# Re-tiling a gated linear attention with a leaky feed-forward into units of one batch and one chunk, with one activation-table set, on one core

## The chip, the core and the metric

The kernel runs on one core of a Trainium2 chip. The metric is the time of one execution on the device, in microseconds (us), where less is better. "Timed" means that figure; "span" means the length of the profiled execution, which is about two us shorter. With one core there is no neighbouring die to compare, so a run counts as slow only when it lies over 1.5% above the fastest of its own kernel.

Engines are named as the profile names them: PE is TensorE's matmul stream, PEld its weight loads, DVE is VectorE, ACT is ScalarE, POOL is GpSimd, SP is SyncE (here it only issues transfers). L89 is line 89 of the kernel concerned. A "unit" below is one batch of one chunk of 128 time steps, with all 8 heads; there are 24 units.

## The reference

```python
# q, k, v, f_logit: (4 batches, 8 heads, 768 steps, 48); all float32
f = 1.0 / (1.0 + np.exp(-f_logit))
for t in range(S):
    state = f[:, :, t, :, None] * state + k_t (outer) v_t      # 48 x 48 per batch and head
    y[:, :, t] = q_t @ state
x = y.transpose(0, 2, 1, 3).reshape(3072, 384)                 # tokens x (heads * 48)
h = x @ w_in                                                   # 384 -> 2048
out = np.maximum(0.01 * h, h) @ w_out                          # 2048 -> 384, float32 out
```

Both kernels work in chunks of 128 steps. Within a chunk, the gates are summed in log space by a matmul with a triangular matrix (`cs`). The queries are then scaled by exp(-cs) and the keys by exp(cs). After a transpose, masked score matmuls (`pw`, `wm`) and a carried state replace the loop over steps.

## The kernel before

One iteration handles one chunk of all 32 batch-head pairs. These are the parts that the argument touches (cuts marked `...`):

```python
    # three per-head tiles, each head padded from 48 to 128 columns
    lf = statep.tile([128, NJ, 128], BF16, tag="lf")           # NJ = 32
    qh = statep.tile([128, NJ, 128], BF16, tag="qh")
    kh = statep.tile([128, NJ, 128], BF16, tag="kh")
    ...
        for kk in range(3):                                    # weights: SyncE loads, ScalarE casts
            stg = wstage.tile([128, FF], FP32, tag="wstg")
            nc.sync.dma_start(out=stg, in_=moe_w_in[kk * 128:(kk + 1) * 128, :])
            nc.scalar.copy(out=w_in_b[:, kk, :], in_=stg)
    ...
        for p in range(4):                                     # emit_attn(c)
            nc.scalar.activation(t_b[:, js, :], f_raw[:, js, :], AF.Exp, scale=-1.0)
            nc.scalar.activation(lf[:, js, 0:D], t_b[:, js, :], AF.Ln, bias=1.0)
            nc.tensor.matmul(cs, ut, lf[:, js, 0:D], start=True, stop=True)
            nc.scalar.activation(a_t[:, js, :], cs, AF.Exp, scale=-1.0)
            nc.scalar.activation(em_t[:, js, :], cs, AF.Exp, scale=1.0)
            ...
        for b in range(4):
            ...                                                # 16 transposes, 8 scores, 16 py per batch
            nc.scalar.copy(out=xnat, in_=py)
            nc.sync.dma_start(out=x_dram[c][b * C:(b + 1) * C, :], in_=xnat)
        ...
        for kk in range(3):                                    # x goes through DRAM to be transposed
            nc.sync.dma_start_transpose(xt, x_dram[c][:, kk * 128:(kk + 1) * 128])

    def emit_moe(c, xts):                                      # 512 tokens at once
        for ff in range(16):
            for kk in range(3):
                nc.tensor.matmul(pm, w_in_b[:, kk, ff * 128:(ff + 1) * 128], xts[kk], ...)
            nc.scalar.activation(gT[:, ff, :], pm, AF.Prelu, alpha=0.01)
        ...
```

Attention of chunk c+1 is emitted before the feed-forward of chunk c.

Of the kernel before, what the change touches and what calls it, by code (L numbers as in the profile page):

```python
# [8 lines left out]
FP32 = mybir.dt.float32  # L10
BF16 = mybir.dt.bfloat16
AF = mybir.ActivationFunctionType


@with_exitstack
def kernel(
# [16 lines left out]
    NJ = B * H  # L33
    KD, FF = moe_w_in.shape

    const = ctx.enter_context(tc.tile_pool(name="const", bufs=1))
    wpool = ctx.enter_context(tc.tile_pool(name="wpool", bufs=1))
    wstage = ctx.enter_context(tc.tile_pool(name="wstage", bufs=1))
    statep = ctx.enter_context(tc.tile_pool(name="statep", bufs=1))
    inp = ctx.enter_context(tc.tile_pool(name="inp", bufs=2))  # L40
    work = ctx.enter_context(tc.tile_pool(name="work", bufs=2))
    xtp = ctx.enter_context(tc.tile_pool(name="xtp", bufs=2))
    gpool = ctx.enter_context(tc.tile_pool(name="gpool", bufs=2))
    opool = ctx.enter_context(tc.tile_pool(name="opool", bufs=4))
    dram = ctx.enter_context(tc.tile_pool(name="dram", bufs=1, space=bass.MemoryType.DRAM))

    ps_cs = ctx.enter_context(tc.tile_pool(name="ps_cs", bufs=1, space=bass.MemoryType.PSUM))
    ps_tp = ctx.enter_context(tc.tile_pool(name="ps_tp", bufs=1, space=bass.MemoryType.PSUM))
    ps_w = ctx.enter_context(tc.tile_pool(name="ps_w", bufs=1, space=bass.MemoryType.PSUM))
    ps_y = ctx.enter_context(tc.tile_pool(name="ps_y", bufs=2, space=bass.MemoryType.PSUM))  # L50
    ps_m = ctx.enter_context(tc.tile_pool(name="ps_m", bufs=3, space=bass.MemoryType.PSUM))
# [7 lines left out]

    state_f = statep.tile([128, NJ, D], FP32, tag="state_f")  # L60
    state_b = statep.tile([128, NJ, D], BF16, tag="state_b")
    nc.vector.memset(state_f, 0.0)
    nc.vector.memset(state_b, 0.0)
    lf = statep.tile([128, NJ, 128], BF16, tag="lf")
    qh = statep.tile([128, NJ, 128], BF16, tag="qh")
    kh = statep.tile([128, NJ, 128], BF16, tag="kh")
    nc.vector.memset(lf[:, :, D:128], 0.0)
    nc.vector.memset(qh[:, :, D:128], 0.0)
    nc.vector.memset(kh[:, :, D:128], 0.0)

    if True:
        w_in_b = wpool.tile([128, 3, FF], BF16, tag="w_in")
        for kk in range(3):
            stg = wstage.tile([128, FF], FP32, tag="wstg")
            nc.sync.dma_start(out=stg, in_=moe_w_in[kk * 128:(kk + 1) * 128, :])
            nc.scalar.copy(out=w_in_b[:, kk, :], in_=stg)
        w_out_b = wpool.tile([128, 16, KD], BF16, tag="w_out")
        for kk in range(4):
            stg = wstage.tile([128, 4, KD], FP32, tag="wstg")
            src = moe_w_out[kk * 512:(kk + 1) * 512, :].rearrange(  # L80
                "(a p) n -> p a n", p=128)
            nc.sync.dma_start(out=stg, in_=src)
            nc.scalar.copy(
                out=w_out_b[:, 4 * kk:4 * kk + 4, :], in_=stg)

    x_dram = [dram.tile([4 * C, KD], BF16, name=f"xdram{c}", tag=f"xdram{c}")
              for c in range(NCH)]

    qv = q.rearrange("b h (nc t) d -> nc t (b h) d", t=C)  # L89
    kv = k.rearrange("b h (nc t) d -> nc t (b h) d", t=C)  # L90
    vv = v.rearrange("b h (nc t) d -> nc t (b h) d", t=C)
    fv = f_logit.rearrange("b h (nc t) d -> nc t (b h) d", t=C)
# [5 lines left out]
    def emit_attn(c):  # L98
        xts_out = []
        q_raw = inp.tile([128, NJ, D], FP32, tag="q_raw")  # L100
        k_raw = inp.tile([128, NJ, D], FP32, tag="k_raw")
        v_raw = inp.tile([128, NJ, D], FP32, tag="v_raw")
        f_raw = inp.tile([128, NJ, D], FP32, tag="f_raw")
        for p in range(4):
            nc.sync.dma_start(out=f_raw[:, 8 * p:8 * p + 8, :],  # L105
                              in_=fv[c, :, 8 * p:8 * p + 8, :], )
        nc.sync.dma_start(out=q_raw, in_=qv[c])
        nc.sync.dma_start(out=k_raw, in_=kv[c])
        nc.sync.dma_start(out=v_raw, in_=vv[c])

        t_b = work.tile([128, NJ, D], BF16, tag="t_b")
        a_t = work.tile([128, NJ, D], BF16, tag="a_t")
        em_t = work.tile([128, NJ, D], BF16, tag="em_t")

        for p in range(4):
            js = slice(8 * p, 8 * p + 8)
            nc.scalar.activation(t_b[:, js, :], f_raw[:, js, :], AF.Exp,  # L117
                                 scale=-1.0)
            nc.scalar.activation(lf[:, js, 0:D], t_b[:, js, :], AF.Ln,  # L119
                                 bias=1.0)  # L120
            cs = ps_cs.tile([128, 8 * D], FP32, tag="cs")
            nc.tensor.matmul(cs, ut, lf[:, js, 0:D], start=True, stop=True)  # L122
            nc.scalar.activation(a_t[:, js, :], cs, AF.Exp, scale=-1.0)  # L123
            nc.scalar.activation(em_t[:, js, :], cs, AF.Exp, scale=1.0)  # L124
            nc.vector.tensor_mul(qh[:, js, 0:D], q_raw[:, js, :],  # L125
                                 a_t[:, js, :])
            nc.vector.tensor_mul(kh[:, js, 0:D], k_raw[:, js, :],  # L127
                                 em_t[:, js, :])

        v_b = work.tile([128, NJ, D], BF16, tag="v_b")  # L130
        nc.scalar.copy(out=v_b, in_=v_raw)  # L131

        if c < NCH - 1:
            csa = ps_cs.tile([128, NJ], FP32, tag="cs")
            for j in range(NJ):
                mm(csa[:, j:j + 1], lf[:, j, :], ones_col, j, NJ)
            A_sb = work.tile([128, NJ], FP32, tag="A_sb")
            nc.scalar.activation(A_sb[0:D, :], csa[0:D, :], AF.Exp,
                                 scale=-1.0)

        qkT = work.tile([128, 2, NJ, 128], BF16, tag="qkT", bufs=1)
        for b in range(4):
            for qk, src in enumerate((qh, kh)):
                tp = ps_tp.tile([128, 8, 128], BF16, tag="tp")
                for hh in range(8):
                    j = 8 * b + hh
                    mm(tp[:, hh, :], src[:, j, :], ident, hh, 8, tr=True)
                nc.vector.tensor_copy(out=qkT[:, qk, 8 * b:8 * b + 8],  # L148
                                      in_=tp)

            wms = []
            for g in range(2):
                pw = ps_w.tile([128, 4, 128], FP32, tag="pw")
                for hh in range(4):
                    j = 8 * b + 4 * g + hh
                    mm(pw[:, hh, :], qkT[:, 1, j, :],
                       qkT[:, 0, j, :], hh, 4)
                wm = work.tile([128, 4, 128], BF16, tag="wm", bufs=4)
                nc.vector.tensor_mul(wm, pw,  # L159
                                     ut[:, None, :].to_broadcast([128, 4, 128]))  # L160
                wms.append(wm)

            py = ps_y.tile([128, 8, D], FP32, tag="py")
            ny = 16 if c > 0 else 8
            if c > 0:
                for hh in range(8):
                    mm(py[:, hh, :], qkT[:, 0, 8 * b + hh, :],
                       state_b[:, 8 * b + hh, :], hh, ny)
            for hh in range(8):
                j = 8 * b + hh  # L170
                mm(py[:, hh, :], wms[hh // 4][:, hh % 4, :], v_b[:, j, :],
                   (ny - 8) + hh, ny)
            xnat = xtp.tile([128, KD], BF16, tag="xnat", bufs=4)
            nc.scalar.copy(out=xnat, in_=py)  # L174
            with tc.high_priority(offset=20000):
                nc.sync.dma_start(out=x_dram[c][b * C:(b + 1) * C, :],
                                  in_=xnat)


        if c < NCH - 1:  # L180
            for b in range(4):
                pt = ps_cs.tile([128, 8, D], FP32, tag="cs", name="pt")
                for hh in range(8):
                    j = 8 * b + hh
                    mm(pt[:, hh, :], kh[:, j, :], v_b[:, j, :], hh, 8)
                ss = slice(8 * b, 8 * b + 8)
                nc.vector.tensor_add(state_f[0:D, ss, :], state_f[0:D, ss, :],
                                     pt[0:D, :, :])
                nc.vector.tensor_mul(
                    state_f[0:D, ss, :], state_f[0:D, ss, :],  # L190
# [70 lines left out]
```

## Time and profile before

| | before |
|---|---|
| timed, median of 4 (range) | 263.91 us (263.54 to 265.58) |
| profiled span | 260.9 us |
| TensorE / ScalarE / VectorE / GpSimd busy | 200.2 / 171.4 / 128.4 / 1.1 us |
| activation-table loads | 35 of 1283 ns = 44.9 us of ScalarE |
| first feed-forward matmul | 62.20 us |

These lines come from the page of the kernel before. The first is busy time with its share of the span. Then come rows of 40 equal slices of the span, each digit the busy share in tenths. Of these, PEclk is the clock granted to TensorE, again in tenths. The chain that ended last follows, then two groups of instructions (count, total busy us, mean ns, then idle time before them).

```profile
PE 200.2 (77%) x1921; PEld 125.9 (48%) x1944; DVE 128.4 (49%) x233; ACT 171.4 (66%) x269; POOL 1.1 (0%) x9
...
PE   0013686016999967955998999996999999999994
...
ACT  3997249994889955899735978469764285505800
...
PEclk9999999555999997995799999999899999999999
...
PE 42%; ACT 33%; DMA 12%; SPq 6%; issue 3%; DVE 2%
...
L119 ACT ACT_TABLE_LOAD x17 | 21.8, 1283 | 0.3
...
L117 ACT ACT_TABLE_LOAD x11 | 14.1, 1283 | 0.2
```

TensorE is busiest over the whole run, but not throughout, and the chain that ended last gives TensorE 42% and ScalarE 33% of the span. TensorE's row is nearly empty (0 1) in the eighth and ninth slices, where ScalarE's row reads 9 9 and the granted clock 5. The windows view says the same in us. Its columns are the stretch, its length, busy us (with instruction count) of PE, PEld, DVE, ACT and POOL, the granted clock, the DMA share (which can pass 1) and GB/s:

```profile
20.00:45.00 25.00, 15.79 (x185) 12.85 (x184) 16.35 (x30) 14.72 (x19) 0.00 (x0) 1.00 0.70 173
45.00:60.00 15.00, 1.97 (x12) 0.72 (x13) 3.63 (x8) 14.55 (x19) 0.00 (x0) 0.51 0.59 101
60.00:80.00 20.00, 18.12 (x164) 10.59 (x167) 8.44 (x15) 14.29 (x23) 0.00 (x0) 0.86 1.04 189
```

From 45 to 60 us TensorE works 1.97 of 15 us while ScalarE works 14.55 us, much of that on table loads: Exp, Ln and the other functions alternate, and each alternation reloads a table. The clock of 0.51 beside that idle stretch agrees with the Trainium skill, "TensorE: Matmul & The Clock Gate", Part 1, which says that the array falls back to half its clock after an idle window of about 3.4 us. As an estimate, TensorE's busy time multiplied by (1 - granted clock), summed over nine windows of the run, gives 11 us of extra matmul time from a lowered clock.

### The profile page before, as it was taken

What the parts mean: (1) busy time and instruction counts of PE and PEld (TensorE: products, weight loads), DVE (VectorE), ACT (ScalarE), POOL (GpSimd) and SP (SyncE); (2) the same over time, 40 slices, a digit from 0 to 9 for tenths busy, and PEclk for the clock granted to TensorE, in tenths of its full rate; (3) what the DMA queues carried; (4) which work ended last, traced back from release to release, by engine and by line L of the source; (5) the groups of instructions that cost most, each with busy time, mean ns of one, the idle gap of its engine ahead of it and who ended that gap; (6) DMA issues with size and microseconds to landing.
All of it is one profiled execution on the core that took longest, in us unless ns stands there. A gap on an engine that the chain in (4) does not pass through costs nothing.

```text
span 260.9 us, 4667 instructions
## 1 busy us (share of the span) xinstructions
PE 200.2 (77%) x1921; PEld 125.9 (48%) x1944; DVE 128.4 (49%) x233; ACT 171.4 (66%) x269; POOL 1.1 (0%) x9
## 2 busy tenths in 40 slices
PE   0013686016999967955998999996999999999994
PEld 0002575003467634743464775654765557564462
DVE  7112759212359854872314995265892387320011
ACT  3997249994889955899735978469764285505800
POOL 1000000000000000000000000000000000000000
PEclk9999999555999997995799999999899999999999
DMA  7990898099599799980999999999002401141011
GB/s 215 191 271 6 228 235 222 23 167 221 102 226 165 135 203 179 139 136 0 169 165 235 199 156 171 184 206 186 18 30 52 136 10 33 33 121 60 3 60 60
DMA packets 118244, 34.90 MB, mean 134 GB/s; under 512 B 109648, under 2 KB 117840, under 8 KB 117840
## 3 DMA queue, kind: packets, MB, share of 16 engines
q1 hardware_dynamic: 118224, 34.61, 68.2%
q8 instruction: 15, 0.25, 0.4%
q14 instruction: 5, 0.04, 0.1%
HBM read 25.17 MB, written 7.08 MB: 124 GB/s over the span
## 4 chain that ended last, share of the span: by engine, by line
PE 42%; ACT 33%; DMA 12%; SPq 6%; issue 3%; DVE 2%
PE pm L208 14%; ACT L119 6%; ACT L117 4%; PE tp L95 4%; DMA stg<-in_moe_w_in_dram 4%; ACT gT L210 3%; ACT lf L119 3%; DMA f_raw<-in_f_logit_dram 3%; ACT a_t L123 3%; SPq L198 3%; ACT t_b L117 3%; SPq L105 2%; ACT em_t L124 2%; PE pw L95 2%; DMA stg<-in_moe_w_out_dram 2%
## 5 line engine op out<-in xcount | busy, mean ns | idle before, releaser
L208 PE MATMUL pm<-xt,w_in_b 128*128 128x512 bf16 x265 | 75.0, 399 | 9.7 <-ACT gT L210 6.3
L210 ACT ACTIVATE gT<-pm 128x512 bf16<-128x512 f32 x96 | 56.4, 601 | 27.0 <-PE pm L208 25.4
L214 PEld LDWEIGHTS <-gT 128*128 128x128 bf16 x384 | 37.0, 98 | 24.4 <-issue 0.5
L159 DVE TENSOR_TENSOR wm<-pw,ut 128x512 bf16<-128x512 f32 x48 | 32.8, 684 | 16.9 <-PE pw L95 16.6
L208 PEld LDWEIGHTS <-w_in_b 128*128 128x128 bf16 x288 | 26.0, 100 | 28.1 <-issue 11.0
L148 DVE COPY qkT<-tp 128x1024 bf16<-128x1024 bf16 x48 | 32.8, 684 | 12.6 <-PE tp L95 12.1
L122 PE MATMUL cs<-lf,ut 128*128 128x384 bf16 x24 | 9.2, 384 | 35.8 <-ACT em_t L124 24.4
L95 PEld LDWEIGHTS <-qkT 128*128 128x128 bf16 x352 | 22.2, 102 | 17.9 <-DVE qkT L148 7.4
L95 PEld LDWEIGHTS <-kh 128*128 128x128 bf16 x352 | 21.8, 105 | 12.1 <-issue 5.6
L125 DVE TENSOR_TENSOR qh<-q_raw,a_t 128x384 bf16<-128x384 f32 x24 | 13.3, 556 | 29.1 <-DMA q_raw<-in_q_dram 17.2
L123 ACT ACTIVATE a_t<-cs 128x384 bf16<-128x384 f32 x24 | 11.9, 494 | 19.3 <-PE cs L122 19.2
L95 PE MATMUL pw<-qkT 128*128 128x128 bf16 x192 | 20.9, 237 | 3.3 <-DVE qkT L148 2.5
L119 ACT ACT_TABLE_LOAD x17 | 21.8, 1283 | 0.3
L95 PE MATMUL tp<-ident,kh 128*128 128x128 bf16 x192 | 17.1, 241 | 1.8 <-DVE kh L127 1.3
L95 PE MATMUL tp<-ident,qh 128*128 128x128 bf16 x192 | 17.2, 239 | 0.0
L122 PEld LDWEIGHTS <-ut 128*128 128x128 bf16 x24 | 2.4, 102 | 29.6 <-issue 25.9
L95 PEld LDWEIGHTS <-qh 128*128 128x128 bf16 x192 | 13.5, 108 | 3.7 <-DVE qh L125 3.5
L174 ACT CAST xnat<-py 128x384 bf16<-128x384 f32 x24 | 11.1, 473 | 6.1 <-PE py L95 5.8
L127 DVE TENSOR_TENSOR kh<-k_raw,em_t 128x384 bf16<-128x384 f32 x24 | 12.7, 552 | 3.9 <-DMA k_raw<-in_k_dram 3.9
L117 ACT ACTIVATE t_b<-f_raw 128x384 bf16<-128x384 f32 x24 | 12.3, 527 | 3.0 <-DMA f_raw<-in_f_logit_dram 2.9
L117 ACT ACT_TABLE_LOAD x11 | 14.1, 1283 | 0.2
L131 ACT CAST v_b<-v_raw 128x1536 bf16<-128x1536 f32 x6 | 8.8, 1468 | 7.1 <-DMA v_raw<-in_v_dram 7.1
(79 smaller groups left out, 211.0 us busy)
## 6 DMA issues: line engine op xcount, KB each, us to landing
f_raw<-in_f_logit_dram SPq DMA_DIRECT2D x24, 192.0 KB, 4.8
q_raw<-in_q_dram SPq DMA_DIRECT2D x6, 768.0 KB, 6.4
k_raw<-in_k_dram SPq DMA_DIRECT2D x6, 768.0 KB, 7.9
v_raw<-in_v_dram SPq DMA_DIRECT2D x6, 768.0 KB, 7.2
out_dram<-osb SPq DMA_DIRECT2D x24, 192.0 KB, 2.1
stg<-in_moe_w_in_dram SPq DMA_DIRECT2D x3, 1024.0 KB, 5.0
stg<-in_moe_w_out_dram SPq DMA_DIRECT2D x4, 768.0 KB, 5.0
xdram_144<-xnat SPq DMA_DIRECT2D x4, 96.0 KB, 2.4
```

The lines of the kernel that those rows point to most:

```text
L95: nc.tensor.matmul(o, l, r, start=(i == 0), stop=(i == n - 1), is_transpose=(True if tr else None))
L117: nc.scalar.activation(t_b[:, js, :], f_raw[:, js, :], AF.Exp, scale=-1.0)
L119: nc.scalar.activation(lf[:, js, 0:D], t_b[:, js, :], AF.Ln, bias=1.0)
L122: nc.tensor.matmul(cs, ut, lf[:, js, 0:D], start=True, stop=True)
L123: nc.scalar.activation(a_t[:, js, :], cs, AF.Exp, scale=-1.0)
L125: nc.vector.tensor_mul(qh[:, js, 0:D], q_raw[:, js, :], a_t[:, js, :])
L127: nc.vector.tensor_mul(kh[:, js, 0:D], k_raw[:, js, :], em_t[:, js, :])
L148: nc.vector.tensor_copy(out=qkT[:, qk, 8 * b:8 * b + 8], in_=tp)
L159: nc.vector.tensor_mul(wm, pw, ut[:, None, :].to_broadcast([128, 4, 128]))
L208: nc.tensor.matmul(pm, w_in_b[:, kk, ff * 128:(ff + 1) * 128], xts[kk], start=(kk == 0), stop=(kk == 2))
L210: nc.scalar.activation(gT[:, ff, :], pm, AF.Prelu, alpha=0.01)
L214: nc.tensor.matmul(pm2, gT[:, ff, nb * 128:(nb + 1) * 128], w_out_b[:, ff, :], start=(ff == 0), stop=(ff == 15))
```

## The change

The intent is to keep TensorE fed with less work on the other engines:

- The work is cut into 24 units of one batch and one chunk.
- Two heads share the partitions (padded to 64 rows each, not 128), so the attention part needs half the transposes.
- The feed-forward runs per unit, two units behind the attention.
- x is transposed by one on-chip DMA transpose, not through DRAM.
- GpSimd loads the weights, casting them on the way.
- One activation-table set is preloaded.

The diff, cut to its core:

```diff
+    nc.scalar.preload_act_table_set("natural_log_exp_and_others")
...
-    lf = statep.tile([128, NJ, 128], BF16, tag="lf")   # and qh, kh
+        lf = const.tile([128, H, 64], BF16, ...)        # three of each in turn
+        qkh = const.tile([128, 2 * H, 64], BF16, ...)
...
-            nc.sync.dma_start(out=stg, in_=moe_w_in[kk * 128:(kk + 1) * 128, :])
-            nc.scalar.copy(out=w_in_b[:, kk, :], in_=stg)
+            nc.gpsimd.dma_start(out=w_in_b[:, kk, :],
+                                in_=moe_w_in[kk * 128:(kk + 1) * 128, :])
...
+    def attn(u):
+        c, b = divmod(u, B)
+        ...                                      # SyncE loads f, q, k, v of this unit
+        if u == 0:
+            load_weights()
+        nc.scalar.activation(t_e, f_raw, AF.Exp, scale=-1.0)
+        nc.scalar.activation(lf[:, :, 0:D], t_e, AF.Ln, bias=1.0)
+        nc.gpsimd.tensor_copy(out=v_b, in_=v_raw)
+        nc.tensor.matmul(cs, ut, lf[:, :, 0:D], start=True, stop=True)
+        nc.scalar.activation(ex[:, 0:H, :], cs, AF.Exp, scale=-1.0)
+        nc.scalar.activation(ex[:, H:2 * H, :], cs, AF.Exp, scale=1.0)
+        nc.vector.tensor_mul(qkh[:, :, 0:D], qk_raw, ex)
+        for i in range(2 * NP):                  # 8 transposes per unit, not 16
+            mm(tp[:, i, :], qkh[:, 2 * i:2 * i + 2, :], ident, i, 2 * NP, tr=True)
+        for p in range(NP):
+            for r in range(2):                   # the two heads of a pair: partitions 0-63, 64-127
+                rs = slice(64 * r, 64 * r + 64)
+                mm(pw[:, r, p, :], qkT[rs, NP + p, :], qkT[rs, p, :], p, NP)
...
-            nc.scalar.copy(out=xnat, in_=py)
-                nc.sync.dma_start(out=x_dram[c][b * C:(b + 1) * C, :], in_=xnat)
-                nc.sync.dma_start_transpose(xt, x_dram[c][:, kk * 128:(kk + 1) * 128])  # x3
+        nc.vector.tensor_copy(out=xnat, in_=py.rearrange("a h d -> a (h d)"))
+        nc.sync.dma_start_transpose(xT, xnat)
...
+    def ffn(u, xT):                              # 128 tokens at once
+        for g in range(4):
+            pm = ps_m.tile([128, 4, 128], FP32, tag="pm")     # two buffers
+            ...                                  # 12 matmuls of 128x128
+            nc.scalar.activation(gT[:, 4 * g:4 * g + 4, :], pm, AF.Prelu, alpha=0.01)
...
+        waiting.append((u, attn(u)))
+        if len(waiting) > DEPTH:                 # DEPTH = 2
+            ffn(*waiting.pop(0))
```

## The prediction

> **What bounds the kernel now.** Span 260.9 us (263.6 timed). First part of the page: TensorE busy 200 us (77%), ScalarE 171 (66%), VectorE 128 (49%), DMA 68%. By the windows view, ScalarE and the loads rule until 60 us (TensorE busy 19 of 60 us; granted clock 0.51 in 45-60 us); from 60 us TensorE is 80-99% busy. Chain of waits: TensorE 42%, ScalarE 33%, DMA 12%. In the groups view, 35 activation-table loads of 1283 ns take 44.9 us of ScalarE.
>
> **What the change does, with durations of this trace.**
> - ScalarE loses 44.9 us of table loads (the Trainium skill, "ScalarE: Activation LUTs", section on table sets, says one set holds both exp and ln; the build has one load), the casts of weights and v (20 us) and of xnat (11 us). Left per unit: three exp and one ln at 0.47-0.5, one tiny exp, four Prelu at 0.6: 4.6 us; all 24: 110 us.
> - TensorE: start to start in the timeline, a 512-wide matmul takes 220 ns, a 384-wide one 163, 128-wide with own weights 55-57, 48-wide 26. So w_in work, 288 x 220 = 63 us, becomes 1152 x 56 = 64: no loss from narrower tiles. (The skill, "TensorE: Matmul & The Clock Gate", back-to-back issue gap, gives 81 ns for such pairs; this trace 57.) w_out stays 63 us. Attention falls from about 57 us to about 40: half the transposes, half the state products, half the column sums. Total issue time 182 -> 167 us, 7.0 us per unit.
> - VectorE per unit: qk product about 0.96 (estimate: 556 ns + 384 columns more), copy 0.68, mask about 1.2, three of 0.55: 4.5 us. GpSimd takes v cast and state[...].
> - The DRAM round trip (landing 2.4 + 2.8 us) becomes one on-chip transpose; the feed-forward trails by a whole unit, so it is hidden.
>
> **Critical path after.** TensorE's order per unit is fixed: cumulative sum, w_in groups 0-1, half of group 2 (waits for Prelu 0, which stands behind both exps), transposes (wait for qk product), scores (wait for copy), last py (waits for mask). These durations give stalls of about 0.5 + 0.15 + 0.15 + 0.15 us, so 8.05 us per unit, TensorE about 87% busy.
> Start: unit 0's feed-forward stands early in TensorE's order, so all waits for the weights: 6.3 MB behind 4-5 MB of inputs at about 220 GB/s (the page's DMA row). I take w_out as complete near 31 us (20-42). Then 21 units x 8.05 = 169, two units without attention 12, tail 3.5 us. Span about 216, timed about 219 us.
>
> **Prediction:** 219 us, range 206 to 238; faster by over 2%: 0.96, within 2%: 0.03, slower: 0.01.
>
> **What would show it right or wrong.** One table load; ScalarE busy about 110 us, VectorE 105-112, TensorE 165-180. Timeline: w_in matmuls 56 ns apart; a period near 8 us per unit, stalls before w_in (Prelu), tp, pw and py. Waits: TensorE's longest on w_in and w_out loads, within 35 us. Issue list: transposes landing in under 4 us, not waited for.
>
> **What would make it wrong.** Casting weight loads from GpSimd slower than 150 GB/s (later start, +10-20 us). Half-height score matmuls draining the array. Single-buffered PSUM tiles or VectorE and GpSimd sharing a port stretching the period above 8.8 us (+18 us). Slow transpose issue on SyncE holding loads back. Weights by 22 us and a 7.5 us period would give 200 us.

## The result

| | before | after |
|---|---|---|
| timed, median of 4 (range) | 263.91 us (263.54 to 265.58) | 221.95 us (221.32 to 222.49) |
| profiled span | 260.9 us | 220.7 us |
| TensorE busy | 200.2 us | 178.7 us |
| ScalarE busy | 171.4 us | 98.7 us |
| VectorE busy | 128.4 us | 105.5 us |
| GpSimd busy | 1.1 us | 50.0 us |
| first feed-forward matmul | 62.20 us | 36.04 us |

The ratio is 0.840 (95% interval 0.837 to 0.844). A ratio compares the fast runs of the two kernels of the same rounds, so it is not quite the ratio of the medians quoted here. The outputs of all twelve experiments below were correct.

The lines of the page of the changed kernel that answer to those of before:

```profile
PE 178.7 (81%) x2376; PEld 135.4 (61%) x2376; DVE 105.5 (48%) x149; ACT 98.7 (45%) x213; POOL 50.0 (23%) x100
...
PE   0000045999798989999999999999999999999993
...
ACT  4000324753744665474556446553744462535440
...
PEclk9999999999999999999999999999999999999999
...
PE 63%; ACT 14%; SPq 12%; DMA 6%; DVE 2%; issue 2%; DVEq 0%; ACTq 0%
```

ScalarE's part of the chain is down to 14% and TensorE's up to 63%, the page records no dip of the granted clock (the last section has a doubt about the start), and TensorE is mostly busy from about 39 us on. Before that, TensorE's row is nearly empty for five slices (27 us). The waits view of the changed kernel says what TensorE waited for there. Each line gives the waiting engine and line, the releaser, total us, how many times, and the longest:

```profile
ACT t_e L109 <- DMA f_raw<-in_f_logit_dram: 33.8, 9, 20.5
...
PE tp L89 <- DVE qkh_88 L119: 22.3, 1, 22.3
...
PE pm L89 <- DMA xT<-xnat: 1.6, 1, 1.6
```

So the longest wait on TensorE is one of 22.3 us at the first transposes. No wait of TensorE for a weight load shows. To see what lay behind the wait, follow it back. The timeline of SyncE's issues (start, duration, what) at the start of the changed kernel:

```profile
0.74 0.44 SPq L98 DMA_DIRECT2D f_raw<-in_f_logit_dram  x1
1.25 0.56 SPq L99 DMA_DIRECT2D qk_raw<-in_q_dram  x1
1.86 0.90 SPq L100 DMA_DIRECT2D qk_raw<-in_k_dram  x1
2.80 5.77 SPq L101 DMA_DIRECT2D v_raw<-in_v_dram  x1
8.61 5.48 SPq L98 DMA_DIRECT2D f_raw<-in_f_logit_dram  x1
14.13 5.16 SPq L99 DMA_DIRECT2D qk_raw<-in_q_dram  x1
19.33 4.18 SPq L100 DMA_DIRECT2D qk_raw<-in_k_dram  x1
23.56 1.40 SPq L101 DMA_DIRECT2D v_raw<-in_v_dram  x1
```

A load of 192 KB that SyncE issues in 0.4 to 0.9 us took it 4.2 to 5.8 us for four loads in a row. That is exactly while GpSimd's weight loads were under way. Those were issued between 1.7 and 5.7 us, and the last landed at about 25 us. The timelines of ScalarE and then TensorE over the same time (the bracket gives the idle time just before and what ended it):

```profile
3.61 0.52 ACT L109 ACTIVATE t_e<-f_raw 128x384 f32<-128x384 f32 x1 [1.59 <-DMA f_raw<-in_f_logit_dram]
4.17 0.52 ACT L110 ACTIVATE lf_87<-t_e 128x384 bf16<-128x384 f32 x1
25.20 0.52 ACT L109 ACTIVATE t_e<-f_raw 128x384 f32<-128x384 f32 x1 [20.51 <-DMA f_raw<-in_f_logit_dram]
25.63 0.47 ACT L117 ACTIVATE ex<-cs 128x384 bf16<-128x384 f32 x1
```

```profile
4.74 0.48 PE L115 MATMUL cs<-lf_87,ut 128*128 128x384 bf16 x1 [4.74 <-ACT lf_87 L110]
27.53 1.03 PE L89 MATMUL tp<-ident,qkh_88 128*128 128x128 bf16 x8 [22.31 <-DVE qkh_88 L119]
```

The sum `cs` of unit 0 was ready at 5.2 us. ScalarE's next instruction in order, however, was unit 1's first exp, whose input landed at 25 us. Unit 0's two exps stood behind it, and with them everything on TensorE. Unit 0's own v was late as well: GpSimd's cast of it started at 23.40 us, after a wait of 16.95 us for the load. So another order on ScalarE alone would have let the transposes begin earlier, but not the products with v.

The steady state is the larger part of the time. This is one whole unit on TensorE, from its cumulative sum to the next one's:

```profile
123.99 0.33 PE L115 MATMUL cs<-lf_91,ut 128*128 128x384 bf16 x1
124.15 2.11 PE L89 MATMUL pm<-xT,w_in_b 128*128 128x128 bf16 x30
126.27 0.62 PE L89 MATMUL tp<-ident,qkh_92 128*128 128x128 bf16 x8
...
127.00 0.72 PE L89 MATMUL pm<-xT,w_in_b 128*128 128x128 bf16 x10
127.68 0.40 PE L89 MATMUL pw<-qkT 64*128 64x128 bf16 x8
...
131.56 0.33 PE L115 MATMUL cs<-lf_95,ut 128*128 128x384 bf16 x1
```

The period is 131.56 - 123.99 = 7.57 us. Ten w_in matmuls with their own weight loads take 0.72 us, of which about 0.22 is the last one's duration, so they start (0.72 - 0.22)/9 = 56 ns apart. Thirty at that pace take 1.84 us, yet the row with thirty took 2.11 us. So 0.27 us is lost somewhere in it. The single starts in the trace say where: the 25th matmul, the first of w_in group 2, starts 329 ns after the 24th, not 56. The transposes start 231 ns after the thirtieth, so another 0.17 us is lost there.

Where the 40.2 us of span came from can be read off one mark, the first feed-forward matmul. It moved from 62.20 to 36.04 us, which is 26.2 us. What follows it shrank from 198.7 to 184.7 us, which is 14.0 us. TensorE's timelines of the kernel before and of the changed kernel, at the mark:

```profile
62.20 0.59 PE L208 MATMUL pm<-xt,w_in_b 128*128 128x512 bf16 x1
```

```profile
36.04 0.80 PE L89 MATMUL pm<-xT,w_in_b 128*128 128x128 bf16 x6 [1.63 <-DMA xT<-xnat]
```

### The profile page after: what moved, and what is told of

The parts are those of the page before. It is cut to its first block, busy times and chain, and to the rows that moved or that the text cites. A ratio compares the mean times of both kernels' runs of the same rounds, so it can differ in the third digit from the quotient of the medians.

```text
span 220.7 us, 5773 instructions
## 1 busy us (share of the span) xinstructions
PE 178.7 (81%) x2376; PEld 135.4 (61%) x2376; DVE 105.5 (48%) x149; ACT 98.7 (45%) x213; POOL 50.0 (23%) x100
## 3 DMA queue, kind: packets, MB, share of 16 engines
q1 hardware_dynamic: 113280, 25.96, 55.9%
q0 software_dynamic: 2544, 3.15, 8.3%
## 4 chain that ended last, share of the span: by engine, by line
PE 63%; ACT 14%; SPq 12%; DMA 6%; DVE 2%; issue 2%; DVEq 0%; ACTq 0%
PE po L89 26%; PE pm L89 18%; PE tp L89 6%; PE py L89 5%; ACT gT L188 5%; ACT ex L117 4%; DMA f_raw<-in_f_logit_dram 4%; SPq L101 4%; PE pw L89 3%; ACT ex L118 3%; SPq L98 3%; SPq L99 3%; SPq L100 3%; PE pt L89 2%; DVE wm L134 2%
## 5 line engine op out<-in xcount | busy, mean ns | idle before, releaser
L89 PE MATMUL pm<-xT,w_in_b 128*128 128x128 bf16 x1152 | 80.4, 220 | 6.6 <-ACT gT L188 3.0
L89 PEld LDWEIGHTS <-w_in_b 128*128 128x128 bf16 x1152 | 68.8, 98 | 14.8 <-issue 11.6
L89 PE MATMUL po<-w_out_b,gT 128*128 128x384 bf16 x384 | 69.9, 326 | 0.0
L117 ACT ACTIVATE ex<-cs 128x384 bf16<-128x384 f32 x24 | 11.7, 490 | 47.1 <-PE cs L115 47.1
L193 DVE COPY osb<-po 128x384 f32<-128x384 f32 x24 | 13.4, 557 | 39.8 <-PE po L89 39.7
L134 DVE TENSOR_TENSOR wm<-pw,ut 128x1024 bf16<-128x1024 f32 x24 | 29.4, 1223 | 3.8 <-PE pw L89 3.1
L125 DVE COPY qkT<-tp 128x1024 bf16<-128x1024 bf16 x24 | 16.6, 691 | 17.2 <-PE tp L89 17.2
L89 PE MATMUL tp<-ident,qkh_88 128*128 128x128 bf16 x64 | 5.4, 231 | 22.4 <-DVE qkh_88 L119 22.3
L112 POOL CAST v_b<-v_raw 128x384 bf16<-128x384 f32 x24 | 13.5, 561 | 40.3 <-DMA v_raw<-in_v_dram 23.0
L119 DVE TENSOR_TENSOR qkh_88<-qk_raw,ex 128x768 bf16<-128x768 f32 x8 | 7.7, 956 | 27.8 <-ACT ex L118 27.8
L147 DVE CAST xnat<-py 128x384 bf16<-128x384 f32 x24 | 13.4, 557 | 11.0 <-PE py L89 10.5
L118 ACT ACTIVATE ex<-cs 128x384 bf16<-128x384 f32 x24 | 11.7, 487 | 0.0
L119 DVE TENSOR_TENSOR qkh_92<-qk_raw,ex 128x768 bf16<-128x768 f32 x8 | 7.7, 958 | 6.5 <-ACT ex L118 6.5
```

Of the source, the lines that this page charges most:

```text
L89: nc.tensor.matmul(o, l, r, start=(i == 0), stop=(i == n - 1), is_transpose=(True if tr else None))
L112: nc.gpsimd.tensor_copy(out=v_b, in_=v_raw)
L117: nc.scalar.activation(ex[:, 0:H, :], cs, AF.Exp, scale=-1.0)
L118: nc.scalar.activation(ex[:, H:2 * H, :], cs, AF.Exp, scale=1.0)
L119: nc.vector.tensor_mul(qkh[:, :, 0:D], qk_raw, ex)
L125: nc.vector.tensor_copy(out=qkT, in_=tp)
```

## The experiments

Twelve kernels were run, each timed in 3 rounds against the kernel before on the same chip (median of the kernel before in those batches: 263.1 to 263.4 us).

### 1. What holds the start: the weights that came too early (w_late)

The theory is that the weight loads, issued before the inputs of the next units, starve the inputs; if they are issued later, TensorE begins earlier. The rival is that the start is a matter of the total of bytes, whatever their order.

```diff
-        if u == 0:
-            load_weights()          # was: before unit 0's exp
...
         nc.gpsimd.tensor_copy(out=v_b, in_=v_raw)
+        if u == 0:
+            load_weights()          # GpSimd issues them once unit 0's v is there
```

> The changed kernel, with the seven weight loads issued from GpSimd only after unit 0's v cast, that is after unit 0's inputs have landed. Theory A (the weight loads[...] crowd out the inputs of units 0 and 1; that is why the first transposes on TensorE start at 27.5 us): first transposes at 7 to 12 us, SyncE's input issues of unit 0 under 1 us each, the cumulative sum of unit 3 (end of the start-up) at 38 to 42 us instead of 46.1, span 4 to 8 us shorter, period unchanged at 7.57 us. Rival B (only the volume counts: the same bytes must land before the feed-forward can run): first transposes earlier but the cumulative sum of unit 3 still at 45 to 48 us, span within 2 us of 220.7.

Measured: 217.88 us (217.59 to 218.41), ratio to before 0.828 [0.825, 0.831], against 0.840 for the change. The first transposes start at 9.63 us rather than 27.53, and the cumulative sum of unit 3 at about 40.8 rather than 46.1. The steady period is unchanged at 7.57 us. SyncE's and TensorE's timelines of this kernel show why an 18 us earlier beginning brought 4 us:

```profile
9.52 8.57 SPq L100 DMA_DIRECT2D qk_raw<-in_k_dram  x1
18.14 5.13 SPq L101 DMA_DIRECT2D v_raw<-in_v_dram  x1
23.31 4.34 SPq L98 DMA_DIRECT2D f_raw<-in_f_logit_dram  x1
27.77 2.46 SPq L149 DMA_TRANSPOSE xT<-xnat  x1
```

```profile
31.69 0.58 PE L89 MATMUL pm<-xT,w_in_b 128*128 128x128 bf16 x4 [14.81 <-DMA xT<-xnat]
```

Unit 0's attention output was ready at about 14.9 us, but its transpose was issued at 27.77. SyncE issues in order and was stuck in three starved loads. The theory holds for the wait that the profile showed. The next wait of the same kind then took its place, and with it most of the gain.

### 2. What sets the period: Prelu or the exps (pm_three, cs_early)

The prediction named "waits for Prelu 0, which stands behind both exps". The rival is the other chain through the same stretch: cumulative sum, two exps, qk product, transposes. The trace can't tell them apart: in the unit shown above, the qk product ran from 125.26 to 126.22 us, and the transposes started at 126.27. So two kernels move them: pm_three takes the Prelu wait away by itself, and cs_early moves the whole chain earlier, and with it the Prelus that stand behind the exps.

pm_three gives the Prelu a third buffer:

```diff
-    ps_m = ctx.enter_context(tc.tile_pool(name="ps_m", bufs=2, space=PSUM))
+    ps_m = ctx.enter_context(tc.tile_pool(name="ps_m", bufs=3, space=PSUM))
-        py = ps_m.tile([128, H, D], FP32, tag="py", bufs=1)
+        py = ps_a.tile([128, H, D], FP32, tag="tp", name="py")   # to make room
```

> The changed kernel with three PSUM buffers for the w_in product instead of two; py takes the bank of the transposes. Theory A (as predicted, the gap of 0.44 us a unit in front of w_in group 2 is a wait for the Prelu that frees its buffer, and costs that much): period 7.15 us, span 8 to 9 us shorter. Rival B (the transposes behind it wait for the exps and the qk product anyway, which end at the same moment): the gap only moves to in front of the transposes, period 7.5 to 7.6 us, span within 1.5 us of the changed kernel.

cs_early puts the sum and what hangs on it earlier in each engine's order:

```diff
-        nc.tensor.matmul(cs, ut, lf[:, :, 0:D], start=True, stop=True)
+        with tc.high_priority(offset=40):
+            nc.tensor.matmul(cs, ut, lf[:, :, 0:D], start=True, stop=True)
...
+        with tc.high_priority(offset=40):          # the two exps and the qk product
```

> The changed kernel with a higher scheduling priority for the cumulative sum, the two exps and the qk product, so that the sum stands some 35 matmuls earlier in TensorE's order and the transposes find their product ready. PSUM buffers as in the changed kernel. Theory A (the chain sum, exps, product, transposes sets the period): gap in front of transposes and group 2 falls from 0.44 to under 0.15 us, period 7.1 to 7.3 us, span 5 to 9 us shorter. Rival B (copy of the transposes and the mask product then bind instead): those two waits grow from 0.1 and 0.1 to 0.4 us or more together, span within 2 us.

Measured: pm_three 220.60 us (219.78 to 222.58), ratio 0.840 [0.835, 0.846], the same ratio as the change. cs_early 217.35 us as the median of four runs, one of which was slow (220.38); its three fast runs lie from 215.48 to 218.41, with the ratio 0.823 [0.817, 0.829]. TensorE's timeline of pm_three:

```profile
129.24 0.33 PE L115 MATMUL cs<-lf,ut 128*128 128x384 bf16 x1
129.40 1.84 PE L89 MATMUL pm<-xT,w_in_b 128*128 128x128 bf16 x30
131.52 0.62 PE L89 MATMUL tp<-ident,qkh 128*128 128x128 bf16 x8 [0.28 <-DVE qkh L119]
```

With three buffers the thirty w_in matmuls take 1.84 us with no gap in them: the Prelu wait is gone. The gap of 0.28 us now stands in front of the transposes, and the period stays at 7.57 us. In cs_early two successive groups of transposes show no gap and the period is 7.19 us (TensorE's timeline, one unit from sum to sum):

```profile
125.71 0.33 PE L117 MATMUL cs<-lf,ut 128*128 128x384 bf16 x1
...
129.20 0.61 PE L90 MATMUL tp<-ident,qkh 128*128 128x128 bf16 x8
...
132.90 0.33 PE L117 MATMUL cs<-lf,ut 128*128 128x384 bf16 x1
```

So the rival was right: with the Prelu wait gone, the chain through the exps and the qk product holds the period where it was. Counted from start to start in the traces, the change loses 0.27 us in front of group 2 and 0.17 in front of the transposes, pm_three loses 0.45 in front of the transposes alone, and cs_early loses nothing at either place, but 0.18 us in front of a later w_in matmul. With smaller differences elsewhere that leaves 7.57 - 7.19 = 0.38 us per unit. This is the price of both waits together. That the chain alone costs so much is not shown: no run moves it and leaves the Prelu wait in place.

### 3. The two heads of a pair (halves_apart)

The prediction feared that score matmuls on half the rows drain the array. The theory tested here was the reverse, that the two halves overlap because they alternate in the program; the rival was that nothing overlaps and the 0.33 us has another source.

```diff
-        for p in range(NP):
-            for r in range(2):
+        for r in range(2):
+            for p in range(NP):
```

> The changed kernel with the eight score matmuls of a unit ordered by half of the array (four on rows 0 to 63, then four on rows 64 to 127) instead of alternating. Theory A (alternating halves overlap: eight in 0.33 us, 41 ns each, against 55 to 57 ns for full-height 128-wide ones): eight take 0.44 to 0.48 us, period up by 0.1 us, span up by 2 to 3 us. Rival B (no overlap; the 0.33 us comes from something else): eight still in 0.33 us, span within 1 us.

Measured: 222.50 us (221.06 to 223.61), ratio 0.845 [0.840, 0.850], not to be told from the change. In the change the eight score matmuls started at 0, 3, 65, 69, 121, 125, 177 and 180 ns, and here at 0, 14, 66, 79, 122, 135, 178 and 191 ns. That is two at a time in either order, against 56 ns for each full-height transpose. So they overlap, against the rival, but the order in the program is not what makes the pairs, against the theory. The trace does not say which matmul each start belongs to. The Trainium skill, "TensorE: Matmul & The Clock Gate", Part 3, "The mechanism", gives about 4 ns between starts on different row groups; the 3 to 4 ns of the change agree, and the 13 to 14 ns of halves_apart do not quite.

### 4. How much is the table set alone (before_one_set, many_sets)

before_one_set is the kernel before with the one line added. many_sets is the changed kernel with it taken out.

```diff
+    nc.scalar.preload_act_table_set("natural_log_exp_and_others")    # before_one_set; minus in many_sets
```

> The kernel before with one line added: the one activation-table set of the change, so one table load instead of 35. Theory A (the loads count where ScalarE rules, in the first 60 us, and hardly after that, where TensorE is 80 to 99% busy): ScalarE busy 128 us, TensorE's first w_in matmul 10 to 20 us earlier than 62 us, total 240 to 252 us. Rival B (every table load is on the path): 215 to 222 us, and the rest of the change is worth nothing. Rival C (TensorE alone sets the time): 258 us or more.

> The changed kernel without its line that fixes the table set: the build has 49 table loads, two a unit, beside the ln. Theory A (ScalarE is under half busy, and the ln is not on the chain, but the Prelus behind it wait): ScalarE busy 160 us, period 7.7 to 8.4 us, total 225 to 242 us. Rival B (all 2.6 us a unit land on the path): period 10 us, total 270 us or more. Rival C (hidden wholly): within 2 us of the changed kernel.

Measured, in one table of two by two (median timed us):

| | old tiling | new tiling |
|---|---|---|
| without the line | 263.38 (same batch) | 244.93 (244.06 to 245.58) |
| with the line | 239.41 (239.13 to 241.88) | 221.95 (another batch; before: 263.91) |

The line is worth 24.0 us on the old tiling and 23.0 on the new. The rest of the change is worth 18.5 without it and 17.5 with it. So the two parts nearly add up, and the larger part of the gain comes from one line. before_one_set just missed its expected ranges: 239.41 us against 240 to 252, and a mark 9.9 us earlier against 10 to 20. The Trainium skill, "ScalarE: Activation LUTs", "Table sets: the hidden batching unit", says that one set holds exp and ln; the trace agrees, with a single load in the changed kernel and 49 in many_sets.

The two traces also say where the rest of the change earns its 17 us. In before_one_set the first feed-forward matmul is at 52.28 us of a span of 237.3, so 185.0 us follow it, against 184.7 in the changed kernel:

```profile
52.28 1.03 PE L210 MATMUL pm<-xt,w_in_b 128*128 128x512 bf16 x2
```

From that mark on, the re-tiled kernel is no faster than the old tiling with one table set, though it has more attention left there (nearly 23 units, where the old tiling has at most 20). What it gains is the mark, 52.28 to 36.04 us: a unit's feed-forward needs one unit of attention and not a whole chunk of four. That this is the reason is argued from the order of the work: no run separates it from the other edits, such as the halved number of transposes.

In many_sets the mark is at 35.32 us, so all the loss comes later: the period is 8.78 us, 1.21 more for two table loads (2.57 us of ScalarE) per unit. ScalarE's and TensorE's timelines:

```profile
125.36 1.28 ACT L107 ACT_TABLE_LOAD   x1
126.66 0.52 ACT L107 ACTIVATE t_e<-f_raw 128x384 f32<-128x384 f32 x1
127.09 0.58 ACT L186 ACTIVATE gT<-pm 128x512 bf16<-128x512 f32 x1
```

```profile
127.72 0.82 PE L87 MATMUL po<-w_out_b,gT 128*128 128x384 bf16 x4 [1.03 <-ACT gT L186]
```

The load delays the last Prelu, and TensorE waits 1.03 us for it, in 12 of the units (12.4 us in all). A period of 7.7 to 8.4 us and a total of 225 to 242 us had been expected; both were missed. ScalarE is 66% busy in this kernel, and it still costs TensorE time because of where in the unit its loads fall.

### 5. The casts on the old tiling (before_set_casts)

On top of before_one_set, GpSimd loads the weights with a cast, and casts v.

```diff
-            nc.sync.dma_start(out=stg, in_=moe_w_in[kk * 128:(kk + 1) * 128, :])
-            nc.scalar.copy(out=w_in_b[:, kk, :], in_=stg)
+            nc.gpsimd.dma_start(out=w_in_b[:, kk, :], in_=moe_w_in[kk * 128:(kk + 1) * 128, :])
...
-        nc.scalar.copy(out=v_b, in_=v_raw)
+        nc.gpsimd.tensor_copy(out=v_b, in_=v_raw)
```

> The kernel before with one table set, and the weights cast by their loads from GpSimd and v cast on GpSimd as in the change; tiles, pairs and round trip as before. Theory A (relief of ScalarE is a part of the gain, the rest is less work on TensorE and a denser order): ScalarE busy 108 us, total 232 to 246 us, so 10 us or more above the changed kernel. Rival B (ScalarE's relief is the whole gain): 218 to 226 us.

Measured: 243.96 us (243.01 to 244.69), ratio 0.926 [0.922, 0.930]. It is 4.6 us slower than before_one_set, although ScalarE's busy time fell from 127.2 to 108.9 us. TensorE does nothing at all from 10 to 20 us, and its first feed-forward matmul moves back from 52.28 to 61.49 us. SyncE's issues of the first q and k took 9.60 and 12.28 us beside the casting loads, so these crowd out the first inputs here as they do in the change; that they cause the whole delay is argued from this timeline, since no run delayed them on the old tiling. From the mark on, 181.4 us follow, against 185.0 in before_one_set. So the relief of ScalarE is worth at most 3.6 us there, and the start lost 9.2. Casts and loads were moved together here, so neither has a figure of its own.

### 6. The on-chip transpose (dram_trip, chip_three, dram_trip_one)

The change transposes x once per unit, 128x384 on chip, 24 times in all. The kernel before stored x to DRAM and read it back by three transposes of 512x128 per chunk, 18 in all. dram_trip takes the changed kernel through DRAM with one store and three transposes of 128x128 per unit, 72 in all, so it is not a return to the kernel before. Theory A was that the trip through DRAM hides behind the distance between a unit's attention and its feed-forward; the rival was that SyncE can't afford the extra transfers.

```diff
-        nc.sync.dma_start_transpose(xT, xnat)
+        nc.sync.dma_start(out=x_d, in_=xnat)                  # dram_trip
+        for kk in range(3):
+            nc.sync.dma_start_transpose(xT[:, kk, :], x_d[:, kk * 128:(kk + 1) * 128])
```

> The changed kernel with x taken through DRAM as before: one store and three 128x128 transposes a unit in place of one on-chip transpose. Theory A (feed-forward trails by a unit of 7.6 us, so a round trip of 5 to 7 us is hidden): period within 0.1 us of 7.57, total 222 to 228 us, the extra in the start-up. Rival B (SyncE waits 2 us for each store to land and issues three transposes of about 1.2 us, which with four loads and a store exceeds the period): SyncE's issue sets a period of 8 us or more, total above 232 us.

dram_trip took 265.92 us (265.56 to 267.44), ratio 1.010 [1.007, 1.014]: it is as slow as the kernel before. Theory A was wrong. Two more kernels separated the trip from the number of transposes:

```diff
+        for kk in range(3):                                   # chip_three: three, no DRAM
+            nc.sync.dma_start_transpose(xT[:, kk, :], xnat[:, kk * 128:(kk + 1) * 128])

+        nc.sync.dma_start(out=x_d, in_=xnat)                  # dram_trip_one: DRAM, one
+        nc.sync.dma_start_transpose(xT, x_d)
```

> The changed kernel with the one on-chip transpose of a unit cut into three of 128x128, still SBUF to SBUF. It tells which half of the slow DRAM trip (265.9 us) is to blame. Theory A (each transpose instruction costs SyncE about 1.2 us whatever its size, but 6.1 us of issue a unit still fits in 7.57): SyncE issues three transposes in about 3.6 us, period 7.57 to 7.8 us, total 222 to 228 us. Rival B (the number of transposes alone sets SyncE's pace): period 9 us or more, total above 250 us.

> The changed kernel with x stored to DRAM and read back by one transpose a unit in place of three. Theory A (store landing of 3 us waited for on SyncE and one transpose of 1.2 us, with 2.5 us of other issues, still fits in 7.57 us): period 7.57 to 8.0 us, total 223 to 233 us. Rival B (the wait of SyncE for the store is what makes the trip slow): period 9 us or more, total above 250 us. If both this run and the one with three on-chip transposes stay near 222, only the sum of the two overruns SyncE.

| kernel | through DRAM | transposes per unit | timed us (range) | first feed-forward matmul | what follows it |
|---|---|---|---|---|---|
| the change | no | 1 | 221.95 (221.32 to 222.49) | 36.04 | 184.7 |
| dram_trip_one | yes | 1 | 225.67 (224.09 to 226.81) | 38.31 | 185.0 |
| chip_three | no | 3 | 244.17 (243.66 to 246.08) | 35.15 | 208.9 |
| dram_trip | yes | 3 | 265.92 (265.56 to 267.44) | 38.43 | 227.3 |

SyncE's timelines, first of the change, then of chip_three and of dram_trip, in the steady state:

```profile
123.26 1.21 SPq L149 DMA_TRANSPOSE xT<-xnat  x1
```

```profile
157.26 4.62 SPq L150 DMA_TRANSPOSE xT<-xnat  x3
```

```profile
157.75 3.65 SPq L153 DMA_TRANSPOSE xT<-xd  x3
```

A transpose of 128x384 costs SyncE 1.21 us to issue, while three of 128x128 cost 3.65 to 4.62 us. Over all transposes of these kernels the median issue is 1.21 us for 128x384 and 1.22 for 128x128, so here it does not depend on the size. All loads, the stores and the transposes share SyncE, in order, so with three per unit the inputs and the transposed x come late. Summed over the traces, SyncE's issues take 127 us in the change, 150 in dram_trip_one, 204 in chip_three and 222 in dram_trip. TensorE's w_in matmuls wait for the transposed x 12 times in chip_three (10.4 us) and 25 times in dram_trip (23.0 us), against once in the change (1.6 us). In dram_trip:

```profile
152.67 1.90 PE L90 MATMUL pm<-xT,w_in_b 128*128 128x128 bf16 x28 [1.03 <-DMA xT<-xd]
```

The trip through DRAM as such costs 3.7 us; of the 2.6 us by which the profiled spans differ, 2.3 lie before the first feed-forward matmul. So in the steady state the number of issues counts, not the latency of the trip. The two costs together (44 us) are more than their sum (22 + 4). SyncE also waits 28.4 us in dram_trip for stores to land, and TensorE's clock falls to 0.95 between its waits. How the remainder divides between these two was not separated. The expectation for chip_three was missed on both sides: it fell between what the theories said.

### 7. The version that beats both (late_and_early, weights_split)

late_and_early joins the edits of w_late and cs_early. weights_split, in addition, loads w_out only with unit 2, to let unit 0's transpose go out sooner.

> Both improvements in one: weight loads after unit 0's inputs, and the higher priority for the cumulative sum, exps and qk product. If the two act in different stages (start-up, steady state) their gains of 4.1 and 4.6 us add: 212 to 215 us, period 7.19. If not, 216 us or more.

> As the run with both improvements, but the w_out loads are issued only after unit 2's v cast, so that the inputs of units 1 and 2 and unit 0's transpose pass between w_in and w_out. Theory (SyncE stands still behind starved input loads while the weights stream, so unit 0's transpose is issued at 28 us though its data is ready at 14 us): the transpose of unit 0 is issued by 22 us, first w_in matmul by 26 us instead of 31.7, total 207 to 212 us. Rival (the volume to be loaded before the third unit, some 8.7 MB, sets the start-up): w_out lands later by as much, total within 2 us of the run with both.

Measured: late_and_early 214.21 us as the median of four runs, one of which was slow (216.64); its three fast runs lie from 213.32 to 214.67, with the ratio 0.814 [0.809, 0.818], 3.2% less than that of the change. weights_split 214.82 us (213.34 to 215.62), ratio 0.816 [0.812, 0.821], the same. By the means of the fast runs, the two gains were 4.0 and 5.2 us apart and 8.0 together, so they nearly add up; in its steady state the period is 7.19 us, but some early units still take 8.1 to 8.8 us. In weights_split unit 0's transpose went out at 20.91 us rather than 28.77, but the first feed-forward matmul came at 28.98 rather than 32.49, and the total did not move: the theory's 207 to 212 us was missed, and the rival's "within 2 us" held. This supports, without proving, that the bytes of weights and first inputs set what is left of the start: this last re-ordering moved the waits about, not the end.

## Why the prediction was right, and which of its steps were not

The total was right: 219 us predicted, 221.95 measured, inside 206 to 238. That it came so close is luck: two terms of the sum missed in opposite directions. With either miss alone it would have been 234 or 210 us, still inside the range.

| term of the span | predicted | measured | difference |
|---|---|---|---|
| start, to the first of the 21 periods | 31 | 46.1 | +15 |
| 21 units with attention | 169 (8.05 each) | 160.0 (7.62 each) | -9 |
| two units without attention | 12 | 11.2 | -1 |
| tail | 3.5 | 3.4 | 0 |
| span | 216 | 220.7 | +5 |

The measured column is TensorE's timeline: the cumulative sum of unit 3 at 46.13, the first feed-forward without attention at 206.12, the last matmul's end at 217.3.

**The start: wrong in mechanism, and 15 us too short.** The step was "unit 0's feed-forward stands early in TensorE's order, so all waits for the weights", with "TensorE's longest on w_in and w_out loads" as its sign. The weights landed by about 25 us, and TensorE's waits for them do not show. What was late were the inputs: four loads took 4.2 to 5.8 us to issue beside the weight transfers, ScalarE's order made unit 0 wait for unit 1's input, and unit 0's own v was there only at about 23.4 us. The prediction listed "slow transpose issue on SyncE holding loads back" as a danger. What happened was the inverse, slow loads holding back the transpose (w_late, 27.77 us). The Trainium skill, "DMA: Bandwidth & Descriptors", "Queues, rings and completion order", says that each DMA engine alternates between queues packet by packet. The trace does not contradict that: 2544 packets of the weight queue carry 3.15 MB, about 1.2 KB each as written, while nearly all of the input queue's 113,280 packets are under 512 bytes. If the profile's packets are what takes turns, which is not shown, the queue with small packets gets less (an estimate from the issue times: four loads of 192 KB in about 20.6 us are 38 GB/s). That the early weights caused the wait for the first units is shown by w_late; that packet size is the reason was only argued.

**The period: 8.05 predicted, 7.57 measured.** The term that was mis-sized is the stalls, along with some of the issue times. The four stalls were put at 0.95 us; counted from start to start in the unit shown above, they are 0.27 + 0.17 + 0.12 + 0.11 = 0.68 us. That leaves 6.9 us of issue where 8.05 - 0.95 = 7.1 had been counted. The half-height score matmuls are one such place: from the start of the scores to what follows takes 0.33 us in the trace, where eight at the prediction's 56 ns make 0.45. The Prelu stall, "about 0.5", measured 0.27, and pm_three showed that removing it alone gains nothing, because the exp and qk chain ends at the same moment; with both waits gone, 0.38 us per unit was gained.

**ScalarE: 110 predicted, 98.7 measured.** The durations were right, but adding them counts overlaps twice: two exps of 0.49 us start 0.39 us apart. On a busy engine, start-to-start distances are what should be added.

**What the change is made of: not asked.** The prediction counted 44.9 us of table loads, 20 of casts, 15 of TensorE issue time and a DRAM trip side by side. The two-by-two table says which counted: the table set 23 to 24 us, everything else 17 to 18, whose parts were not measured one by one. Moving the casts and the weight loads to GpSimd cost 4.6 us on the old tiling (before_set_casts). On the new tiling a DRAM trip would cost 3.7 us, and a transpose cut into three 22; the second is no part of the gain, since the kernel before issued only 18 transposes. The prediction had called the transpose hidden and given SyncE's issue time no term.

**What was right.** The w_in matmuls lose nothing by being 128 columns wide (56 ns apart, as predicted). The qk product takes 956 to 958 ns (0.96), the mask 1223 ns (about 1.2). VectorE is busy 105.5 us (105 to 112), TensorE 178.7 us (165 to 180). There is one table load. The transposes land in 2.8 us as the median (under 4) and are waited for only at unit 0, for 1.6 us. TensorE bounds the steady state: it waits about 0.7 of 7.57 us there.

## What to carry to other kernels

Check a prediction term by term, not by its total: here 15 us too little in the start and 9 us too much in the period left a total that looked exact. When two waits end at the same instant, the profile can't say which binds; take one away by itself, and read whether the gap vanishes or only moves. A large weight load issued early on a second queue can starve the small loads of the first units, and an engine's issue time is a resource like any other: hold the weights until the first inputs are there, and count transposes by the instruction, not by the byte.

## What the Trainium skill lacked or had wrong

- "DMA: Bandwidth & Descriptors", "Issuing engines are not separate DMA queues", calls the sequencer time of initiating a DMA "usually small relative to the DMA itself". Here a transpose costs SyncE 1.21 us to issue, against 2.8 us from issue to landing, and three of a third of the size 3.65 to 4.62 us. That difference was worth 22 us in 222. The page has no time for issuing a transpose from SyncE on this chip: a dispatch time stands only in its breakdown for GpSimd's DMAs, and cycle counts per instruction only where it sets trn3 beside "previous generations".
- The same page describes the turns that queues take but not what they do to an issuing engine: the issue of a 192 KB load stretched from 0.4 to 0.9 us to 4.2 to 5.8 us (8.57 us at worst, in w_late) beside weight loads of another queue.
- "ScalarE: Activation LUTs", "What ACT_TABLE_LOAD costs", has 1283 ns, which the trace shows, plus a drain of about 1380 ns. No such drain is visible: in many_sets a load that starts at 125.36 us is followed by its activation at 126.66, 1.30 us later, and the two loads per unit lengthened the period by 1.21 us.
- "TensorE: Matmul & The Clock Gate", "Back-to-back issue gap", gives 81 ns per matmul of 128 columns when each has its own weight load, and 56 ns as the isolated gap. The trace shows 56 ns in such a stream (thirty in 1.84 us in pm_three).
- The same page warns that clock records can't always be trusted; none says how it shows in a page of this kind. In the changed kernel PEclk reads 9 throughout, yet the first eight transposes took 1.03 us, against 0.62 us for the same eight later on; in the trace most of them start 107 ns apart, against 56 later. In that stretch the spacing is the better sign of a slow clock.
